# A Fourier transform and a two-layer network on one core: the first batch in two wide chunks instead of three narrow ones

## The chip, the core and the metric

The kernel runs on one NeuronCore of a Trainium2 chip. The core has five engines with a queue of their own each, which run side by side and wait for one another through semaphores: TensorE (matrix multiplications into PSUM; PE in the profile, its weight loads PEld), VectorE (DVE), ScalarE (ACT), GpSimd (POOL) and SyncE (SP), which here only issues DMAs. Every engine works through its instructions in the order in which the program gives them. The metric is the device time of one execution in microseconds (us); lower is better.

## The reference

```python
X = np.fft.fft(np.fft.fft(x, axis=1), axis=2)      # x: 8 x 3008 x 256, float32
x = X.real.astype(np.float32).reshape(8 * 3008, 256)
h = x @ w_in                                       # 256 x 2048
g = np.maximum(0.01 * h, h)
return (g @ w_out).astype(np.float32)              # 2048 x 256
```

The real part of a two-dimensional Fourier transform (over sequence and features) of eight batches, then a linear layer, a leaky ReLU and a second linear layer for each of the 24064 rows. The weights arrive as 64-bit floats.

## The kernel before

**Transform.** Each batch is transformed along the sequence in two units, the odd rows and the even rows of the result (`units`; 753 and 752 columns in all). A unit is made by folding the input (sums and differences, "x folds"), small matmuls against tables, and a butterfly of sums on VectorE into `mix_sb`; a separate row for the middle ("Nyquist") feature goes through DRAM and is broadcast into `nb_sb`. The feature transform is folded into `w_in`, which gives `wf`.

**Columns.** The first 504 columns of batch 0 are done by plain steps: sixteen pairs (j, f), `steps`, where `raised` (R) makes the hidden sums of two hidden blocks in four PSUM half banks, `activate` (A) adds the middle row, makes sum and difference on VectorE and the leaky ReLU on ScalarE, and `down_plain` (D0 and D1, the two halves of the output) multiplies by `wo`. A Lrelu of an A inside the first chunk is not issued at once but put into the list `waiting`, and goes out after the next up.

All other columns are done by chunks (`Chunk`). Each has 16 "ups" (`up`, L1235: one matmul for the cosine and one for the sine part over the chunk's width w), with the cosine bank seeded beforehand by ScalarE (`seed`, L1230), copied out by ScalarE (L1241) and combined with the sine bank by VectorE (`hidden`, L1248, two operations, the "hidden pair"), then a Lrelu (L1511). Then a fast multiplication scheme: 28 sums of the hidden values on VectorE and GpSimd (`sum`, L1265), 26 products of four matmuls with n = w/2 columns (`product`, L1286), and combinations on VectorE (L1332). The weights of the products are sums of `w_out` blocks, made by GpSimd (W, L736), stored to DRAM (L741) and streamed back (L760).

**Order.** Nothing is left to a scheduler: every engine gets its instructions in program order. `HEAD` is a written list of operations ahead of the first chunk. `rest` then sorts events by a step number: chunk t has its ups at steps 16t + 1.2 + f and its products from 16t + 18.1 on, beside the next chunk's ups. `START` is a table of further operations at the beginning of steps. The background work for the next batches (`work`, x folds and transforms) is put in by budgets per step (`SHARES`). The letters of `HEAD` and `START` mean: L load a weight part; C finish converting one part from 64-bit floats and begin the next (B, M, E are pieces of it); S and F fold a quarter of `w_in` into `wf` (S two sums, F matmuls on TensorE, L708, and four ScalarE copies, L712); T, N, NF tables and the middle row; W the weight sums of one group.

A conversion C is five VectorE operations (L651, L643, L644, L660, L661); the two ScalarE ones of the part that is begun (L645, L646) wait for L644.

**Banks.** Ups use `cos_ps` and `sin_ps`, two banks each. In the first chunk, for the ups f < `EARLY`, `half` gives bank 0 alone, since the plain steps and F use bank 1; then the two alternate. `seed_next` seeds the next up only after the copy of this one while f < `EARLY`. Where a chunk is wider than all before it, `touch` (L1226) first runs a small matmul over the new columns of both banks.

**Before, batch 0:** the chunks have 248, 380 and 373 columns (n = 124, 190, 187); the transform of its second unit is done inside the first chunk (in `start_work`, steps 5 to 13), which holds only columns of the first unit. All other batches have three chunks of 504, 504 and 497. That makes 24 chunks.

Of the kernel before, what the change touches and what calls it, by code (L numbers as in the profile page):

```python
# [16 lines left out]
P = 128  # L17
# [23 lines left out]
CW = 252  # L41
# [21 lines left out]
    15: "D0:15",  # L63
    16: "D1:15",
    17: "",
# [4 lines left out]
L:o3 D0:0 R:1 B:o1 D1:0 A:2 R:3 C:o1 A:1 A:3 D0:2 L:w2a C:w1a C:w1b D1:2 D0:1 L:w2b S:1 D1:1 D0:3 F:1 D1:3 R:4 C:o2 L:o4 L:o5 A:4 C:o3 R:5 A:5 D0:4 C:w2a D1:4 R:6 L:w3a A:6 D1:5 T C:w2b D0:5 R:7 D0:6 A:7 S:2 L:w3b L:o6 F:2 C:o4 D1:6 R:8 A:8 N D1:7 R:9 C:o5 D0:7 A:9 R:10 NF C:w3a D0:8 A:10 L:o7 D0:9 C:w3b R:11 S:3 D1:9 W:1 D1:8 W:0 A:11 F:3  # L70
"""
EARLY = 14
FIRST_DOWN = 18.1
FIRST_PER = 6.5
RF = 128
SHARES = (0.9, 1.2, 1.34)
DIRECT = (11, 13)
WORK_FROM = 14
FOLDS_FROM = 16
FIRST = 125  # L80
# [54 lines left out]
SECOND = 380  # L135
# [195 lines left out]
def tile_fnet_leaky_relu(  # L331
# [41 lines left out]
    def ring(tag):  # L373
# [5 lines left out]
    assert weights_at >= lay_out(block_sb, 0, (("win", 4, WN), ("power", 2, WN), ("raw", 1, 2 * WN), ("e", 2, 2 * WN), ("o", 2, 2 * WN),  # L379
                                               ("g", 5, 2 * WN), ("s", 4, 2 * WN)))  # L380
# [96 lines left out]
    def turn(x, y, a, part, tmp, to, v, sc=None):  # L477
# [4 lines left out]
        if v is folds:  # L482
# [110 lines left out]
    feat_sb = in_parts(2 * 2 * P, 2, 2 * P, where="cos")  # L593
# [15 lines left out]
    RAW = "o e raw o e o e raw o e o e raw o e raw".split()  # L609
# [117 lines left out]
    def weight(w):  # L727
        if w >= 8:
            return wt[:, w - 8]
# [46 lines left out]
    stream = Stream()  # L776
    reach = [w % 4 for w in range(8)]
    for x_, y_, _ in W_SUMS:
        reach.append(max(reach[x_], reach[y_]))

# [277 lines left out]
    class Later:  # L1058
# [4 lines left out]
        def __init__(self):  # L1063
            self.queue, self.turn, self.alone = [], 0, 0
# [65 lines left out]
    class Slots:  # L1130
# [3 lines left out]
        def __init__(self):  # L1134
            self.under = {SLOTS + i: {4 * RF * i // SS, (4 * RF * (i + 1) - 1) // SS} for i in range(16)}
            self.free = set(range(SLOTS)) - set().union(*self.under.values())
# [16 lines left out]
        def drop(self, i):  # L1153
            if i in self.under:
                freed = self.under.pop(i)
                self.free |= freed - set().union(*self.under.values())
            else:
                self.free.add(i)

        def place(self, i, n):  # L1160
            if i >= SLOTS:
                return block_sb[:, (i - SLOTS) * 4 * RF : (i - SLOTS + 1) * 4 * RF].rearrange("p (g n) -> p g n", g=4)[:, :, 0:n]
            return block_sb[:, i * SS : i * SS + 4 * RS].rearrange("p (g n) -> p g n", g=4)[:, :, 0:n]

        def row(self, r, g, n):
            if r[0] >= SLOTS:
                all_of = block_sb[:, 0 : 64 * RF].rearrange("p (i n) -> p i n", n=4 * RF)
                return all_of[:, r[0] - SLOTS : r[-1] + 1 - SLOTS, g * RF : g * RF + n]
# [32 lines left out]
    class Chunk:  # L1201
# [18 lines left out]
        def half(self, f):  # L1220

            return 0 if self is every[0] and f < EARLY else f % 2

# [8 lines left out]
        def up(self, f):  # L1232
# [5 lines left out]
            if g == 0:  # L1238
                self.at.update(zip(range(4 * k, 4 * k + 4), block.take_four() if self is not every[0] else range(SLOTS + 4 * k, SLOTS + 4 * k + 4)))
# [122 lines left out]
    def step_of(b, i, r):  # L1362

        return 16 * (3 * b + i) + r
# [53 lines left out]
    def rest():  # L1418
# [99 lines left out]
    def start_work(r):  # L1518
# [4 lines left out]
        if r == 5:  # L1523
            store_weights(range(8))
        if r in (6, 7):
            store_weights([8 + i for last in ((1, 0), (2, 3))[r - 6] for i in range(len(W_SUMS)) if reach[8 + i] == last])
        if r == 10:
            stream.load_to(5)
        if r == 17:
            stream.load_to(RING)  # L1530
        if r in (5, 7):
            part = (r - 5) // 2
            fold_halves(t, part, 0, slice(0, 2 * FI))
            evens.append(Direct(t[:, part, 0, :, part * P : (part + 1) * P], part, even_tables[part], 0))
        if r in (8, 10):
            evens[(r - 8) // 2].fold_odd(t[:, (r - 8) // 2, 1, 0:2, 0:P])
        if r == 9:
            rings["dft"] = rings["up"]
            nyq_t = nyquist_tile()
            made = butterfly(nyquist_halves(nyq_t, 0), B, 0, 0)  # L1540
            made[0](even_rows(nyq_of[0], B))
            made[1](odd_rows(nyq_of[0], B))
            store_nyquist(0, nyq_t)
            spread(1)
        if r in DIRECT:
            dft_direct(DIRECT.index(r))

# [11 lines left out]
    def do(op, later=None):  # L1559
# [36 lines left out]
        elif kind == "NF":  # L1596
# [4 lines left out]
            nyq_of.append(rows)  # L1601
        else:
# [146 lines left out]
```

## Time and profile before

| | us |
|---|---|
| median of 3 runs (lowest, highest) | 1816.27 (1816.03, 1816.39) |
| profiled execution, its own time | 1816.45 |
| its span, from the first to the last instruction | 1814.3 |
| TensorE busy in the span | 1806.7 |
| VectorE busy | 1537.6 |
| ScalarE busy | 1065.0 |
| GpSimd busy | 1036.3 |
| first up of chunk 0, 1, 2, 3 begins at | 94.3, 138.6, 181.1, 239.0 |

A row of the timeline has the start, the time to the end of the last of the merged instructions, engine, line, operation, output and inputs, shape, count, and in brackets the idle time ahead of it and what ended it. A matmul of 32-bit floats appears as two records, and the end of a record is modelled: the next matmul starts before it. So the cost of a matmul is read from one start to the next.

### The profile page before, as it was taken

What the parts mean: (1) busy time and instruction counts of PE and PEld (TensorE: products, weight loads), DVE (VectorE), ACT (ScalarE), POOL (GpSimd) and SP (SyncE); (2) the same over time, 40 slices, a digit from 0 to 9 for tenths busy, and PEclk for the clock granted to TensorE, in tenths of its full rate; (3) what the DMA queues carried; (4) which work ended last, traced back from release to release, by engine and by line L of the source; (5) the groups of instructions that cost most, each with busy time, mean ns of one, the idle gap of its engine ahead of it and who ended that gap; (6) DMA issues with size and microseconds to landing.
All of it is one profiled execution on the core that took longest, in us unless ns stands there. A gap on an engine that the chain in (4) does not pass through costs nothing.

```text
span 1814.3 us, 23376 instructions
## 1 busy us (share of the span) xinstructions
PE 1806.7 (100%) x7512; PEld 1358.3 (75%) x7512; DVE 1537.6 (85%) x2684; ACT 1065.0 (59%) x1891; POOL 1036.3 (57%) x461
## 2 busy tenths in 40 slices
PE   9999999999999999999999999999999999999999
PEld 7788877777777777777777777777777777777778
DVE  8879988897788987999878989689887997886868
ACT  4768666665556655666556655566555665555540
POOL 0156656565566655755656656566566566565730
PEclk9999999999999999999999999999999999999999
DMA  7366454533454333633436234443443533323324
GB/s 249 108 236 220 135 166 140 176 112 101 132 175 143 121 99 116 214 99 125 130 122 203 90 121 135 149 159 100 133 131 130 175 120 118 121 90 104 126 90 153
DMA packets 148872, 252.49 MB, mean 139 GB/s; under 512 B 18944, under 2 KB 55424, under 8 KB 148752
## 3 DMA queue, kind: packets, MB, share of 16 engines
q1 hardware_dynamic: 148608, 251.02, 42.0%
q8 instruction: 60, 0.98, 0.2%
q14 instruction: 60, 0.49, 0.1%
q10 hardware_dynamic: 144, 0.00, 0.0%
HBM read 219.41 MB, written 31.54 MB: 138 GB/s over the span
## 4 chain that ended last, share of the span: by engine, by line
PE 96%; DVE 3%; issue 0%; POOL 0%; ACT 0%; DVEq 0%; POOLq 0%
PE sum_psc L1286 21%; PE sum_psa L1286 17%; PE sum_psb L1286 17%; PE cos_psa L1235 9%; PE sin_psa L1235 9%; PE cos_psb L1235 8%; PE sin_psb L1235 8%; PE dft_ps L813 3%; DVE block L1265 1%; PE sum_psa L1610 1%; PE dft_ps L1050 1%; DVE block L1026 0%; PE sum_psb L1050 0%; PE sum_psc L1050 0%; PE sum_psa L1050 0%
## 5 line engine op out<-in xcount | busy, mean ns | idle before, releaser
L1265 POOL TENSOR_TENSOR block<-block 128x1008 f32<-128x1008 f32 (+4 forms) x414 | 996.1, 2417 | 640.4 <-DVE xt L1071 172.0
L1286 PE MATMUL sum_psc<-block,wr 128*128 128x252 f32 (+4 forms) x1912 | 428.0, 367 | 0.1
L1286 PEld LDWEIGHTS sum_psc<-block,wr 128*128 128x128 f32 x1912 | 353.8, 190 | 92.2 <-issue 58.2
L1265 DVE TENSOR_TENSOR block<-block 128x1008 f32<-128x1008 f32 (+4 forms) x258 | 415.7, 1615 | 0.3
L1511 ACT ACTIVATE block<-block 128x504 f32<-128x504 f32 (+7 forms) x556 | 399.0, 747 | 4.4 <-DVE block L1248 4.2
L1248 DVE TENSOR_TENSOR block<-cos,sin_psa 128x504 f32<-128x504 f32 (+4 forms) x398 | 238.5, 640 | 148.9 <-PE sin_psa L1235 145.6
L1286 PE MATMUL sum_psb<-block,wr 128*128 128x252 f32 (+4 forms) x1536 | 349.5, 367 | 0.0
L1286 PE MATMUL sum_psa<-block,wr 128*128 128x252 f32 (+4 forms) x1544 | 346.3, 367 | 0.1
L1286 PEld LDWEIGHTS sum_psb<-block,wr 128*128 128x128 f32 x1536 | 282.4, 190 | 83.6 <-issue 53.5
L1286 PEld LDWEIGHTS sum_psa<-block,wr 128*128 128x128 f32 x1544 | 285.1, 190 | 66.4 <-issue 38.8
L1248 DVE TENSOR_TENSOR block<-cos,sin_psb 128x504 f32<-128x504 f32 (+4 forms) x370 | 228.3, 658 | 92.8 <-PE sin_psb L1235 90.7
L1241 ACT COPY cos<-cos_psa 128x504 f32<-128x504 f32 (+4 forms) x199 | 110.2, 554 | 257.9 <-PE cos_psa L1235 257.9
L1241 ACT COPY cos<-cos_psb 128x504 f32<-128x504 f32 (+4 forms) x185 | 105.0, 567 | 228.1 <-PE cos_psb L1235 227.9
L1235 PE MATMUL cos_psa<-mixc,wf 128*128 128x504 f32 (+4 forms) x398 | 190.6, 561 | 0.5 <-ACT cos_psa L1230 0.5
L1235 PE MATMUL sin_psa<-mixs,wf 128*128 128x504 f32 (+4 forms) x398 | 190.5, 560 | 0.0
L1332 DVE TENSOR_TENSOR part<-part 128x252 f32<-128x252 f32 (+4 forms) x357 | 187.8, 563 | 1.4
L1235 PE MATMUL cos_psb<-mixc,wf 128*128 128x504 f32 (+4 forms) x370 | 182.2, 574 | 0.0
L1235 PE MATMUL sin_psb<-mixs,wf 128*128 128x504 f32 (+4 forms) x370 | 182.2, 574 | 0.0
L1235 PEld LDWEIGHTS sin_psa<-mixs,wf 128*128 128x128 f32 x398 | 75.4, 190 | 82.5 <-issue 63.2
L1230 ACT ACTIVATE cos_psa<-nb,small 128x504 f32<-128x504 f32 (+4 forms) x199 | 131.2, 659 | 7.5 <-PE cos_psa L1226 1.2
L1235 PEld LDWEIGHTS sin_psb<-mixs,wf 128*128 128x128 f32 x370 | 70.3, 190 | 81.7 <-issue 66.1
L1230 ACT ACTIVATE cos_psb<-nb,small 128x504 f32<-128x504 f32 (+4 forms) x185 | 124.5, 673 | 7.1 <-PE cos_psb L1226 1.2
(203 smaller groups left out, 1348.1 us busy)
## 6 DMA issues: line engine op xcount, KB each, us to landing
wr<-w_dram SPq DMA_DIRECT2D x600, 256.0 KB, 3.4
xt<-in_x_dram SPq DMA_DIRECT2D x28, 1024.0 KB, 7.3
out_dram<-part SPq DMA_DIRECT2D x112, 126.0 KB, 1.8
out_dram<-part SPq DMA_DIRECT2D x56, 124.5 KB, 1.9
tabe<-in_seq_tab_dram SPq DMA_DIRECT2D x29, 190.0 KB, 3.9
w_dram<-block SPq DMA_DIRECT2D x18, 256.0 KB, 3.6
block<-in_w_in_dram SPq DMA_DIRECT2D x8, 512.0 KB, 4.7
block<-in_w_out_dram SPq DMA_DIRECT2D x8, 512.0 KB, 4.5
```

The source lines that it names most:

```text
L813: nc.tensor.matmul(o, lhsT=still, rhs=moving, start=(i == 0), stop=(i == 3), skip_group_check=True)
L1050: nc.tensor.matmul(sums[j][d][:, r * n : (r + 1) * n], lhsT=wo[:, fs[h] // 4, fs[h] % 4, d], rhs=a[r][h], start=(f == 0 and r == 0 and h = ...
L1230: nc.scalar.activation(cos_ps[self.half(f)][:, 0 : self.w], nb_sb[:, self.lo : self.lo + self.w], ACT.Copy, scale=wn[:, f : f + 1])
L1235: nc.tensor.matmul(bank[:, 0 : self.w], lhsT=wf[:, i, f * P : (f + 1) * P], rhs=mix_sb[i][:, self.lo : self.lo + self.w], start=(i == 1), ...
L1241: nc.scalar.copy(copy, cos[:, 0 : self.w])
L1248: nc.vector.tensor_tensor(block.row(to, g, self.n), x, y, op=op)
L1265: ins = (engine or nc.gpsimd).tensor_tensor(self.value(16 + i), xa, ya, op=ALU.add if sign > 0 else ALU.subtract)
L1286: nc.tensor.matmul(to, lhsT=stream.weight(self.t, q, g), rhs=self.value(v)[:, g], start=(first and at == 0), stop=(last and g == 3), skip_ ...
L1332: ins = nc.vector.tensor_tensor(part_of[self.copy[v]][:, 0:n], xa, ya, op=ALU.add if sign > 0 else ALU.subtract)
L1511: nc.scalar.activation(to, to, ACT.Lrelu)
L1610: nc.tensor.matmul(pt[:, 0:columns], lhsT=blank[:, 0:P], rhs=blank[:, 0:columns], start=True, stop=True)
```

## The change

Batch 0 gets two chunks of 504 and 497 columns like the other batches (23 chunks in all). The first one now begins in unit 0 and ends in unit 1, so the second unit's transform (Q, Y and X, formerly in `start_work`) moves into `HEAD`. In exchange the last quarter of `w_in` (C:w3a, C:w3b, S:3, F:3) moves from `HEAD` into the first steps of the first chunk, and the plain steps R:12 to R:15 with their A and D move some steps back. The load of batch 1's input goes from step 14 to step 1, and its folds begin at step 8. Up f = 4 of the first chunk uses bank 1 (`ASIDE`). The hidden values of the first chunk lie in ordinary slots of `block_sb` (`FIRST_SLOTS`), and the head's buffers there are laid out anew. Until step 17 the x folds use no PSUM copies (`folds.copies`): both inputs are in SBUF. The weight sums are stored in two parts, at steps 3 and 11. The diff is cut to what the prediction speaks of.

```diff
 START = {
-    0: "C:o6 D0:10 R:12 A:12",
-    1: "D1:10 M:o7",
-    2: "R:13 A:13",
-    3: "D0:11 E:o7 D1:11 W:2 W:3",
-    4: "R:14 A:14",
-    5: "D0:12",
-    6: "R:15 A:15",
-    7: "D1:12",
-    8: "D0:13",
-    9: "D1:13",
-    10: "D0:14",
-    12: "D1:14",
-    15: "D0:15",
+    0: "C:w3a D0:10",
+    1: "L:o7 D1:10",
+    2: "C:w3b D0:11",
+    3: "S:3 D1:11",
+    4: "F:3",
+    5: "C:o6",
+    6: "M:o7 E:o7",
+    7: "R:12 A:12 W:3",
+    8: "D0:12",
+    9: "D1:12",
+    10: "R:13 A:13",
+    11: "R:14 A:14",
+    12: "D0:13",
+    13: "D1:13 D0:14",
+    14: "R:15 A:15",
+    15: "D1:14 D0:15",
     16: "D1:15",
-    17: "",
 }
...
-... D1:7 R:9 C:o5 D0:7 A:9 R:10 NF C:w3a D0:8 A:10 L:o7 D0:9 C:w3b R:11 S:3 D1:9 W:1 D1:8 W:0 A:11 F:3
+... D1:7 R:9 C:o5 D0:7 A:9 R:10 NF Q:0 D0:8 A:10 Q:1 W:2 D0:9 R:11 Y D1:9 A:11 X:0 D1:8 X:1
...
-EARLY = 14
+EARLY, ASIDE = 14, 4
-SHARES = (0.9, 1.2, 1.34)
-DIRECT = (11, 13)
-WORK_FROM = 14
-FOLDS_FROM = 16
+SHARES = (2.4, 1.6, 1.34)
+WORK_FROM = 1
+FOLDS_FROM = 8
...
+FIRST_SLOTS = [(14, 15, 16, 17), (10, 11, 12, 13), (6, 7, 8, 9), (18, 19, 20, 21)]
...
-    ends = [PLAIN * CW, UW[1], UW[1] + SECOND, sum(UW)]
-    for lo, hi in zip(ends, ends[1:]):
-        add(0, lo, hi)
-    for b in range(1, B):
-        for lo in range(0, sum(UW), WIDE):
+    for b in range(B):
+        for lo in range(0 if b else PLAIN * CW, sum(UW), WIDE):
             add(b, lo, min(lo + WIDE, sum(UW)))
...
         def by_turns(self, to, x, y, op):
             self.turn = (self.turn + 1) % TURNS
+            if not self.copies:
+                return self.tensor_tensor(to, x, y, op)
...
-            return 0 if self is every[0] and f < EARLY else f % 2
+            return int(f == ASIDE) if self is every[0] and f < EARLY else f % 2
...
-        return 16 * (3 * b + i) + r
+        return 16 * (3 * b + i - 1) + r
...
-                now[0] = SHARES[0] if 16 * t + i < 34 else SHARES[1] if 16 * t + i < 48 else SHARES[2]
+                now[0] = SHARES[0] if 16 * t + i < 17 else SHARES[1] if 16 * t + i < 32 else SHARES[2]
...
-        if r == 5:
+        if r == 3:
+            store_weights([w for w in by_reach if reach[w] == 2])
+        if r == 8:
             store_weights(range(8))
-        if r in (6, 7):
-            store_weights([8 + i for last in ((1, 0), (2, 3))[r - 6] for i in range(len(W_SUMS)) if reach[8 + i] == last])
-        if r == 10:
+        if r == 11:
+            store_weights([w for w in by_reach if reach[w] == 3])
+        if r == 13:
             stream.load_to(5)
         if r == 17:
+            folds.copies = True
+            block.free |= block.later
             stream.load_to(RING)
-        if r in (5, 7):
...
+        elif kind == "Q":
+            part = int(at)
+            fold_halves(t, part, 0, slice(0, 2 * FI))
+            evens.append(Direct(t[:, part, 0, :, part * P : (part + 1) * P], part, even_tables[part], 0))
+            evens[part].fold_odd(t[:, part, 1, 0:2, 0:P])
+        elif kind == "X":
+            dft_direct(int(at))
+        elif kind == "Y":
+            pt = raw[steps[PLAIN * NH - 5]]
+            assert cos_ps[0] in pt
+            rings["dft"] = [0, [i for i in rings["up"][1] if i not in pt]]
...
+            store_nyquist(0, nyq_t)
+            spread(1)
```

More of the change, by code (lines that the diff above doesn't have):

```diff
@@ L481, in turn @@
         sc = nc.scalar if sc is None else sc
-        if v is folds:
+        if v is folds and folds.copies:
             tmp = [misc_ps[0:ROWS, (2 * a + i) % 4 * P : ((2 * a + i) % 4 + 1) * P] for i in range(2)]
@@ L779, in tile_fnet_leaky_relu @@
         reach.append(max(reach[x_], reach[y_]))
+    by_reach = sorted(range(8, len(reach)), key=lambda w: reach[w])
+    stream = Stream()
     def even_rows(rows, m):
@@ L1063, in __init__ @@
         def __init__(self):
-            self.queue, self.turn, self.alone = [], 0, 0
+            self.queue, self.turn, self.alone, self.copies = [], 0, 0, False
         def tensor_tensor(self, to, x, y, op):
@@ L1134, in __init__ @@
         def __init__(self):
-            self.under = {SLOTS + i: {4 * RF * i // SS, (4 * RF * (i + 1) - 1) // SS} for i in range(16)}
-            self.free = set(range(SLOTS)) - set().union(*self.under.values())
+            self.free = set(range(FIRST_SLOTS[3][3] + 1, SLOTS))
+            self.later = set(range(FIRST_SLOTS[2][0]))
         def take(self):
@@ L1238, in up @@
             if g == 0:
-                self.at.update(zip(range(4 * k, 4 * k + 4), block.take_four() if self is not every[0] else range(SLOTS + 4 * k, SLOTS + 4 * k + 4)))
+                self.at.update(zip(range(4 * k, 4 * k + 4), block.take_four() if self is not every[0] else FIRST_SLOTS[k]))
             copy = cos_sb[:, f % 2, 0 : self.w]
```

46 lines of the change are left out of this document (11 added, 35 removed).

## The prediction, made before the changed kernel was run

> **What bounds the kernel now.** I read the page first, then busy time by stage, then TensorE in order of time around the first chunks. Times are us, from the span's start.
>
> ```profile
> span 1814.3 us, 23376 instructions
> PE 1806.7 (100%) x7512; PEld 1358.3 (75%) x7512; DVE 1537.6 (85%) x2684; ACT 1065.0 (59%) x1891; POOL 1036.3 (57%) x461
> PE 96%; DVE 3%; issue 0%; POOL 0%; ACT 0%; DVEq 0%; POOLq 0%
> ```
>
> TensorE is the chain. A change can win only by taking matmul time away or by removing its gaps, and it loses where it makes gaps. The first chunk (up matmuls from 94.27) and everything from the first chunk of batch 1 on, in the view of stages:
>
> ```profile
> 94.27:139.00 44.73, 44.05 (x215) 37.49 (x214) 32.74 (x78) 28.11 (x60) 24.54 (x19) 1.00 0.69 243
> 239.00:1814.00 1575.00, 1571.72 (x6348) 1166.14 (x6346) 1330.30 (x2256) 905.96 (x1585) 933.22 (x376) 1.00 0.40 132
> ```
>
> From 239 on TensorE never stands, though DVE (third figure) is busy 84% of it. That part isn't edited, so the difference is made before it. The gaps there, in TensorE's timeline:
>
> ```profile
> 130.20 0.58 PE L1235 MATMUL sin_psa<-mixs,wf 128*128 128x248 f32 x2
> 131.32 0.69 PE L1235 MATMUL cos_psa<-mixc,wf 128*128 128x248 f32 x2 [0.54 <-ACT cos_psa L1230]
> ...
> 134.51 0.58 PE L1235 MATMUL sin_psa<-mixs,wf 128*128 128x248 f32 x2
> 135.13 0.49 PE L1226 MATMUL cos_psa<-mixc,wf 128*128 128x132 f32 x2
> 135.46 1.86 PE L1050 MATMUL sum_psb<-block,wr 128*128 128x252 f32 x8
> ```
>
> The first pair shows the pattern that decides my forecast. The first chunk keeps to one pair of banks, so an up waits until ScalarE has copied the cosine bank and seeded it anew (L1230); without other matmuls between two ups TensorE stands. Only 0.5 of such waiting is in the profile now.
>
> **Removed: narrow chunks.** Product matmuls (two records each), starts of consecutive groups:
>
> ```profile
> 168.65 1.50 PE L1286 MATMUL sum_psb<-block,wr 128*128 128x124 f32 x12
> 169.99 0.39 PE L1286 MATMUL sum_psc<-block,wr 128*128 128x124 f32 x2
> ...
> 236.75 1.46 PE L1286 MATMUL sum_psb<-block,wr 128*128 128x190 f32 x8
> 238.04 1.13 PE L1286 MATMUL sum_psc<-block,wr 128*128 128x190 f32 x6
> ...
> 307.98 3.14 PE L1286 MATMUL sum_psa<-block,wr 128*128 128x252 f32 x14
> ...
> 310.95 1.01 PE L1235 MATMUL cos_psa<-mixc,wf 128*128 128x504 f32 x2
> ```
>
> A record costs 1.34/12 = 0.1117 at 124 columns, 1.29/8 = 0.161 at 190, 2.97/14 = 0.212 at 252. The columns are the same before (124 + 190 + 187 = 501) and after (252 + 249). From 190 to 252 a column costs 0.00082, so 187 costs 0.1588 and 249 costs 0.2097. Three chunks: 0.4315; two: 0.4217. The 0.0098 is saved 208 times: 2.0. The ups keep their 1002 columns and lose 64 records at the fixed few ns, within that figure's rounding. **-2.0.**
>
> The touches (L1226) run where a chunk is wider than all before it; now the first is the widest, so all four go. Each costs 135.46 - 135.13 = 0.33 and the gap ahead, here 135.13 - (134.51 + 0.42) = 0.2, elsewhere 0.1 to 0.26: **-2.0** for four. The wait at 130.62 goes with the narrow chunk (0.7, and two delayed issues of 0.1): **-0.9**. Together -4.9.
>
> **Moved, costed near nothing.** The second unit's transform (Q, Y, X) goes from the first chunk into the head with its matmuls unchanged; the last quarter's fold and R:12 go the other way. Unit 1's final sums must now be ready before the first up:
>
> ```profile
> 121.27 1.44 PE L554 MATMUL cos_psb<-block,xt 128*128 128x378 f32 x6
> ...
> 123.84 0.58 PE L1235 MATMUL cos_psa<-mixc,wf 128*128 128x248 f32 x2
> ```
> ```profile
> 124.57 0.67 DVE L887 TENSOR_TENSOR mixc<-half,sin_psb 128x189 f32<-128x189 f32 x3
> ```
>
> One X is 2.57 on TensorE, and VectorE ends 1.4 behind it. D0:10 and D1:10 (1.70 each, eight records of 0.212) stand between X:1 and the first up, and cover that; without them it would cost 1.4. The nyquist row's store and broadcast have D1:9, X:0, D1:8 and X:1 (8.5) as cover. For odd issue delays **+0.3**, bounds 0 and 1.4. On SyncE's queue, the input of batch 1 (from step 14 to 1) and the first weight sums' stores (step 3) go ahead of the small copies behind F:3:
>
> ```profile
> 104.58 13.07 SPq L741 DMA_DIRECT2D w_dram<-block  x18
> ```
>
> Seven stores issue in 7 x 0.73 = 5.1, well before A:12 needs those copies in step 7. The first x folds have 7 steps for their load. The later half of batch 1's first transform falls into the second chunk, whose load is like that of the stage from 239 on: 0, bounds 0 and +1.
>
> **Moved, and not covered: the waits in the first wide chunk.** Its steps have TensorE work as the new table lists it: 16 ups, ten half-downs, four R and F:3. The prices at the new width are in the later chunks:
>
> ```profile
> 302.59 1.01 PE L1235 MATMUL cos_psa<-mixc,wf 128*128 128x504 f32 x2
> 303.44 1.01 PE L1235 MATMUL sin_psa<-mixs,wf 128*128 128x504 f32 x2
> 303.63 0.58 ACT L1241 COPY cos<-cos_psa 128x504 f32<-128x504 f32 x1 [1.45 <-PE cos_psa L1235]
> 304.25 0.69 ACT L1230 ACTIVATE cos_psa<-nb,small 128x504 f32<-128x504 f32 x1
> ...
> 305.38 1.04 ACT L1511 ACTIVATE block<-block 128x1008 f32<-128x1008 f32 x1
> ...
> 306.21 1.25 DVE L1248 TENSOR_TENSOR block<-cos,sin_psa 128x504 f32<-128x504 f32 x2
> ```
>
> An up is 2 x 0.845 = 1.69. The copy starts 1.04 after the cosine half and takes 0.58, the seed 0.69, a Lrelu 1.0, the hidden pair 1.25 (1.18 to the next). F and a conversion stand in the head, on TensorE, ScalarE and VectorE:
>
> ```profile
> 47.15 1.02 PE L708 MATMUL cos_psb<-block,cos 128*128 128x512 f32 x2
> ...
> 52.03 1.12 PE L1005 MATMUL sin_psa<-mixc,wf 128*128 128x252 f32 x4 [0.40 <-ACT sin_psa L997]
> ```
> ```profile
> 47.35 1.19 ACT L712 COPY wf<-sin_psa 64x512 f32<-64x512 f32 x2 [1.75 <-PE sin_psa L708]
> 48.44 1.17 ACT L712 COPY wf<-cos_psb 64x512 f32<-64x512 f32 x2
> 49.64 0.72 ACT L645 ACTIVATE block<-block,small 128x512 f32<-128x512 int32 x1
> 50.39 0.72 ACT L646 ACTIVATE block<-block,small 128x512 int32<-128x512 f32 x1
> 51.02 0.96 ACT L997 ACTIVATE sin_psa<-nb,small 128x252 f32<-128x252 f32 x2
> ```
> ```profile
> 46.78 0.69 DVE L651 SCALAR_TENSOR_TENSOR wr<-block,wr 128x512 f32<-128x512 uint32 x1
> ...
> 48.78 0.69 DVE L661 SCALAR_TENSOR_TENSOR wr<-wr,block 128x512 f32<-128x512 f32 x1
> ...
> 50.82 0.86 DVE L1018 SCALAR_TENSOR_TENSOR part<-nb,small,sin_psb 128x252 f32<-128x252 f32 x2 [1.35 <-PE sin_psb L1005]
> 51.79 1.27 DVE L1026 TENSOR_TENSOR block<-part,cos_psa 128x504 f32<-128x504 f32 x2
> ```
>
> So a C is 2.6 on VectorE, its two Relus 1.4 on ScalarE, F's four copies 2.2, an A 2.1 on VectorE. Here, too, the seed (L997) came behind copies and Relus, and TensorE waited at 52.03 although half-downs and an R lay between. I follow the three queues by these prices, with 0 at the first wide up:
>
> - *Step 3, 0.5.* C:w3b runs on VectorE 3.2 to 5.8; its Relus keep ScalarE until 5.95, so copy 1 and seed 2 end at 7.2, and up 2 could have begun at 6.8.
> - *Step 5, 1.45.* F:3 ends at 10.9. Behind its copies (to 12.7) stand copy 3 and seed 4, to 13.95. TensorE has only up 3, done at 12.6.
> - *Step 6, 2.95.* C:o6 waits on VectorE behind hidden pair 3 (to 14.55); its Relus end at 17.35, copy 4 and seed 5 at 18.6. Up 4 was done at 15.75, and steps 5 and 6 hold no half-down and no R.
> - *Step 8, 2.65.* E:o7 and hidden pair 5 hold VectorE to 22.3, A:12 to 24.45; its Lrelu, behind that of pair 5, ends at 26.35. D0:12 reads it, one step after A:12 instead of five; up 6 ended at 23.8.
> - *Step 15, 1.6.* A:15's Lrelu, behind two seeds and another Lrelu, ends at 55.05; D1:14 ended at 53.6.
>
> With 0.25 for small delays these give **+9.4**. Each row's duration is measured; that the order of the queues makes them add is worked out. Its bounds are 0 (ScalarE and VectorE are covered after all) and 12 (with the port, below).
>
> **Sum.** -4.9 + 0.3 + 9.4 = +4.8. The profiled execution took 1816.45, 2.15 of it outside the span; that makes 1821.25, and the median of the runs is 0.18 under it: **1821.0**.
>
> **Rivals.** *(1) ScalarE isn't late: faster.* If the Relus of C:w3b and C:o6 and F's copies come early enough that seed 4 and seed 5 are no more than half a us late, and D0:12 finds its Lrelu, only about 1.5 of waiting is left: 1816.27 - 4.9 + 0.3 + 1.5 = 1813.2. For it: half-downs and R cover ten of sixteen steps, and now nearly all is covered. Against it: steps 5 and 6 have nothing on TensorE but one up each. *(2) One wait pays for the next: no change.* While TensorE stands in steps 5 and 6 VectorE catches up, and the Lrelus ahead of D0:12 and D0:15 are done in time. 9.4 - 2.65 - 1.6 = 5.2 remain: 1816.9. Against it: A:12 comes behind E:o7 on VectorE, not behind TensorE. *(3) The port: slower still.* The x folds start in step 8 without their PSUM copies, so both inputs are in SBUF, while GpSimd makes the last eleven weight sums (W:3 in step 7). What that can cost, with GpSimd's sums beside the first row and not beside the second:
>
> ```profile
> 113.07 1.99 DVE L571 TENSOR_TENSOR xt<-xt 128x128 f32<-128x128 f32 x2
> ...
> 120.63 0.47 DVE L571 TENSOR_TENSOR xt<-xt 128x128 f32<-128x128 f32 x2
> ```
>
> That is 0.76 more for one operation. Eight folds in steps 8 and 9 would be 6 later on VectorE; half lies under the wait for D0:12 and the half-downs, so hidden pair 8 comes some 2.5 late: 1823.5. The Trainium skill, page "SBUF — State Buffer", section "SBUF: two separate sides", says why: VectorE with two SBUF inputs and GpSimd take the shared port in turn, each for a whole instruction. By that rule every one of these folds may wait out a GpSimd sum; the two rows agree with it.
>
> **Chances.** Forecast 0.44, (1) 0.12, (2) 0.31, (3) 0.13. A difference under 0.2% (3.6) can't be told from none. Faster takes (1) less its upper edge: 0.10; slower takes (3) and the forecast's part over 1819.9: 0.54; the rest, 0.36, is within. The forecast's own range is 1818 to 1823; the range 1813.5 to 1824.5 holds most of (1) and (3) too.
>
> **What would show it.** Right: in the first chunk TensorE idle before cos_psb and cos_psa (L1235), released by the seed L1230, of 1 to 3 us at the fifth and sixth up, and before sums (L1050) released by the Lrelu L1511; no L1226; 0 lost later. Wrong: less than 4 us of idle between the first up and the second chunk, or fresh idle in the head or the second chunk, where I count 0.3 and 0. The forecast fails first if the seeds of the fifth and sixth up come in time.

## The result, and the profile after

The changed kernel takes **1833.13 us** (median; lowest 1832.31, highest 1833.41), the kernel before 1816.38 in runs on the same chip. The ratio is 1.0091, 95% interval 1.0076 to 1.0106: slower by 16.7. The prediction, 1821.0 with a range of 1813.5 to 1824.5, had the direction and little over a quarter of the size.

The page of the changed kernel, and its view of stages for the first chunk (ups from 103.3 to 170.4) and for everything from batch 1's first chunk on (columns as before: TensorE, weight loads, VectorE, ScalarE, GpSimd, granted clock, DMA share, GB/s):

```profile
span 1830.5 us, 22511 instructions
PE 1808.5 (99%) x7232; PEld 1336.7 (73%) x7232; DVE 1543.0 (84%) x2608; ACT 1046.2 (57%) x1791; POOL 1034.6 (57%) x443
PE 93%; DVE 4%; ACT 1%; DMA 1%; issue 1%; SPq 0%; POOL 0%; DVEq 0%; POOLq 0%
```
```profile
103.30:170.40 67.10, 56.41 (x181) 34.35 (x181) 58.38 (x88) 45.16 (x66) 20.17 (x14) 0.97 0.60 206
244.10:1830.00 1585.90, 1582.95 (x6347) 1172.99 (x6345) 1337.18 (x2251) 904.52 (x1561) 949.85 (x380) 1.00 0.40 131
```

TensorE, 96% of the chain before, is 93% of it now. In the first chunk it stands 67.10 - 56.41 = 10.7 us, and in what remains the granted clock is 0.97; the later stage is as it was. So the loss lies in the head and the first chunk. TensorE's timeline there, the rows with a wait ahead of them (in brackets; "issue": none that the profile shows) and three without:

```profile
91.35 1.98 PE L550 MATMUL sin_psa<-block,xt 128*128 128x378 f32 x6 [3.67 <-issue]
...
110.58 1.11 PE L1225 MATMUL cos_psa<-mixc,wf 128*128 128x504 f32 x2 [0.30 <-ACT cos_psa L1220]
...
117.52 1.11 PE L1225 MATMUL cos_psb<-mixc,wf 128*128 128x504 f32 x2 [1.57 <-ACT cos_psb L1220]
...
122.07 1.20 PE L1225 MATMUL cos_psa<-mixc,wf 128*128 128x504 f32 x2 [2.60 <-ACT cos_psa L1220]
123.06 1.89 PE L1225 MATMUL sin_psa<-mixs,wf 128*128 128x504 f32 x2
124.74 1.83 PE L1002 MATMUL cos_psb<-mixc,wf 128*128 128x252 f32 x4
126.41 1.01 PE L1002 MATMUL sin_psb<-mixs,wf 128*128 128x252 f32 x4
...
131.55 1.97 PE L1047 MATMUL sum_psa<-block,wr 128*128 128x252 f32 x8 [2.44 <-ACT block L1501]
...
139.55 1.11 PE L1225 MATMUL sin_psa<-mixs,wf 128*128 128x504 f32 x2 [1.80 <-DVE block L1238]
...
143.66 1.11 PE L1225 MATMUL sin_psa<-mixs,wf 128*128 128x504 f32 x2 [0.46 <-DVE block L1238]
...
145.81 1.12 PE L1002 MATMUL sin_psb<-mixs,wf 128*128 128x252 f32 x4 [0.18 <-DVE block L1023]
...
163.53 1.97 PE L1047 MATMUL sum_psa<-block,wr 128*128 128x252 f32 x8 [1.34 <-ACT block L1501]
...
174.52 1.10 PE L1225 MATMUL sin_psb<-mixs,wf 128*128 128x498 f32 x2 [1.01 <-DVE block L1238]
```

Five of these waits are the five that the prediction named (steps 3, 5, 6, 8 and 15), at their places and released by the engines it named. Four things are beside them.

*The head, 91.35.* Ahead of X stands a wait of 3.67. VectorE's fold of the second unit (L440) in its two halves, Q:0 and Q:1, and the first two and the last two of GpSimd's seven weight sums W:2, of which all but the first run beside the second half:

```profile
78.58 0.95 DVE L440 TENSOR_TENSOR xt<-xt 128x768 f32<-128x768 f32 x1
...
82.12 7.65 DVE L440 TENSOR_TENSOR xt<-xt 128x768 f32<-128x768 f32 x1
```
```profile
80.33 2.51 POOL L732 TENSOR_TENSOR block<-wr 128x512 f32<-128x512 f32 x2
...
86.46 2.50 POOL L732 TENSOR_TENSOR block<-block,wr 128x512 f32<-128x512 f32 x2
```

The same operation takes 0.95 alone and 7.65 beside the sums, and it ends only when GpSimd has done all seven (88.96). The two operations just ahead of it, with one input in PSUM (L1023, 80.94), take 1.27 beside the first sums and 1.27 without them (77.39). Y's operations on VectorE are queued behind it, and X waits for them.

*The granted clock.* Three of the five-us stretches (the last but two columns is the clock):

```profile
85.00:90.00 5.00, 2.67 (x18) 1.98 (x15) 4.97 (x2) 1.14 (x4) 3.96 (x4) 1.00 0.00 0
90.00:95.00 5.00, 3.65 (x10) 2.83 (x11) 4.00 (x14) 1.42 (x3) 0.00 (x0) 0.72 0.03 5
...
120.00:125.00 5.00, 2.93 (x5) 1.42 (x6) 3.91 (x7) 4.61 (x8) 0.26 (x1) 0.80 0.25 67
```

After the wait in the head, and again after those of steps 5 and 6, TensorE runs at half speed for a while: above, the sine half begun at 123.06 takes 124.74 - 123.06 = 1.68 instead of 0.845, and the four records after it 1.67 instead of 0.85. Each such stretch costs 1.7. In the profile of before there is none after its first six us.

*Steps 9 to 11, 139.55.* The x folds (L1068) with both inputs in SBUF, five beside GpSimd's last weight sums and five without them:

```profile
130.40 7.91 DVE L1068 TENSOR_TENSOR xt<-xt 128x512 f32<-128x512 f32 x5
...
150.18 3.10 DVE L1068 TENSOR_TENSOR xt<-xt 128x512 f32<-128x512 f32 x5
```

0.96 more for each. *The second chunk, 174.52.* The turn (L1090), two operations on VectorE that also read SBUF twice, beside three block sums of GpSimd:

```profile
168.48 3.68 DVE L1090 SCALAR_TENSOR_TENSOR xt<-xt,small 95x128 f32<-95x128 f32 x2
```
```profile
167.35 8.12 POOL L1255 TENSOR_TENSOR block<-block 128x1008 f32<-128x1008 f32 x3 [26.68 <-PE sin_psa L1225]
```

The parts are counted on TensorE's records: from each start to the next, less what a record of that many columns takes in an undisturbed row (0.4225 at 504, 0.2125 at 252). Matmul time falls by 2.9, and the small waits of before at 130 to 139 and 232 to 237 (2.0) go. Against these -4.9 stand 5.4 in the head (3.7 of waiting, 1.7 at half clock), 9.6 in the five waits with their delayed issues, 1.7 at half clock behind steps 5 and 6, 3.2 in steps 9 to 11 and 1.3 in the second chunk: together **+16.3**; the span grew by 1830.5 - 1814.3 = 16.2. (The profiled execution is the shortest of the five, 1832.31.)

### The profile page after: what moved, and what is told of

Its sections match the earlier page's. It is cut to its first block, busy times and chain, and to the rows that moved or that the text cites. A ratio compares the mean times of both kernels' runs of the same rounds, so it can differ in the third digit from the quotient of the medians.

```text
span 1830.5 us, 22511 instructions
## 1 busy us (share of the span) xinstructions
PE 1808.5 (99%) x7232; PEld 1336.7 (73%) x7232; DVE 1543.0 (84%) x2608; ACT 1046.2 (57%) x1791; POOL 1034.6 (57%) x443
## 4 chain that ended last, share of the span: by engine, by line
PE 93%; DVE 4%; ACT 1%; DMA 1%; issue 1%; SPq 0%; POOL 0%; DVEq 0%; POOLq 0%
PE sum_psc L1276 21%; PE sum_psa L1276 17%; PE sum_psb L1276 17%; PE cos_psa L1225 8%; PE sin_psa L1225 8%; PE sin_psb L1225 8%; PE cos_psb L1225 8%; PE dft_ps L810 3%; DVE block L1255 1%; PE sum_psa L1605 1%; DVE block L1238 1%; DVE xt L1068 0%; DVE block L1023 0%; DMA w_dram<-block 0%; DVE part L1322 0%
## 5 line engine op out<-in xcount | busy, mean ns | idle before, releaser
L1255 POOL TENSOR_TENSOR block<-block 128x1008 f32<-128x1008 f32 (+1 forms) x396 | 994.2, 2522 | 633.2 <-DVE xt L1068 162.2
L1276 PE MATMUL sum_psc<-block,wr 128*128 128x252 f32 (+1 forms) x1832 | 425.9, 375 | 0.2 <-DVE block L1255 0.2
L1255 DVE TENSOR_TENSOR block<-block 128x1008 f32<-128x1008 f32 (+1 forms) x248 | 416.0, 1682 | 0.1
L1501 ACT ACTIVATE block<-block 128x504 f32<-128x504 f32 (+3 forms) x510 | 393.3, 798 | 2.7 <-DVE block L1238 2.4
L1238 DVE TENSOR_TENSOR block<-cos,sin_psa 128x504 f32<-128x504 f32 (+1 forms) x380 | 239.5, 671 | 159.0 <-PE sin_psa L1225 154.8
L1276 PE MATMUL sum_psb<-block,wr 128*128 128x252 f32 (+1 forms) x1472 | 346.9, 376 | 0.0
L1276 PE MATMUL sum_psa<-block,wr 128*128 128x252 f32 (+1 forms) x1480 | 344.9, 375 | 0.0
L1238 DVE TENSOR_TENSOR block<-cos,sin_psb 128x504 f32<-128x504 f32 (+1 forms) x356 | 224.2, 671 | 96.2 <-PE sin_psb L1225 94.8
L1225 PE MATMUL sin_psa<-mixs,wf 128*128 128x504 f32 (+1 forms) x380 | 192.1, 587 | 2.3 <-DVE block L1238 2.3
L1225 PE MATMUL cos_psa<-mixc,wf 128*128 128x504 f32 (+1 forms) x380 | 191.3, 585 | 2.9 <-ACT cos_psa L1220 2.9
```

Of the source, the lines that this page charges most:

```text
L1225: nc.tensor.matmul(bank[:, 0 : self.w], lhsT=wf[:, i, f * P : (f + 1) * P], rhs=mix_sb[i][:, self.lo : self.lo + self.w], start=(i == 1), ...
L1238: nc.vector.tensor_tensor(block.row(to, g, self.n), x, y, op=op)
L1255: ins = (engine or nc.gpsimd).tensor_tensor(self.value(16 + i), xa, ya, op=ALU.add if sign > 0 else ALU.subtract)
L1276: nc.tensor.matmul(to, lhsT=stream.weight(self.t, q, g), rhs=self.value(v)[:, g], start=(first and at == 0), stop=(last and g == 3), skip_ ...
L1501: nc.scalar.activation(to, to, ACT.Lrelu)
```

## The experiments

The theories: **(A)** GpSimd's weight sums shut out VectorE's operations with two SBUF inputs (the port), and each long gap costs half-clock time on top; **(B)** the late seeds of ScalarE, behind the conversions, F and E, make the first-chunk waits; **(C)** VectorE simply has too much to do in the first chunk, so that what is taken from one place comes back at another. Time lost on TensorE is in all 8.7 before and 28.0 after, by the count above; the matmuls that e2 adds (2.1) are not counted as lost.

| run | median (lowest to highest) | ratio, 95% interval | lost on TensorE |
|---|---|---|---|
| the change | 1833.13 (1832.31, 1833.41) | 1.0091 (1.0076, 1.0106) | 28.0 |
| e1 sums behind Y | 1826.84 (1826.31, 1827.12) | 1.0056 (1.0041, 1.0071) | 22.0 |
| e2 gap filled | 1832.82 (1831.62, 1833.16) | 1.0088 (1.0073, 1.0103) | 26.7 |
| e3 sums at step 10 | 1835.17 (1833.91, 1836.28) | 1.0102 (1.0087, 1.0117) | 32.0 |
| e4 weights in the head | 1826.33 (1825.54, 1828.57) | 1.0058 (1.0041, 1.0075) | 21.2 |
| e5 spread | 1823.98 (1823.61, 1824.37) | 1.0042 (1.0027, 1.0057) | 20.2 |
| e6 all in the head | 1822.90 (1822.67, 1825.83) | 1.0041 (1.0026, 1.0055) | 18.6 |
| e7 late turn | 1824.75 (1823.66, 1826.38) | 1.0046 (1.0031, 1.0061) | 21.3 |
| e8 copies covered | 1822.14 (1820.25, 1823.02) | 1.0030 (1.0018, 1.0041) | 18.9 |
| e9 turn in PSUM | 1821.40 (1819.58, 1822.67) | 1.0024 (1.0014, 1.0035) | 17.3 |
| e10 fewer folds at 8 | 1820.82 (1819.33, 1822.34) | 1.0023 (1.0014, 1.0032) | 17.0 |
| e11 border | 1820.91 (1820.42, 1821.34) | 1.0023 (1.0014, 1.0032) | 16.9 |
| e12 folds at 7 | 1819.50 (1819.21, 1821.43) | 1.0018 (1.0009, 1.0027) | 16.6 |

**e1, the weight sums W:2 behind Y.**

```diff
-... Q:0 D0:8 A:10 Q:1 W:2 D0:9 R:11 Y D1:9 A:11 ...
+... Q:0 D0:8 A:10 Q:1 D0:9 R:11 Y W:2 D1:9 A:11 ...   # GpSimd's first sum waits for Y's last VectorE operation
```

> The first seven weight sums on GpSimd (W:2) wait for the last VectorE operation of Y instead of running beside Q:1. If the long fold in Q:1 (7.65 us against 0.95 in Q:0) is VectorE shut out by those sums, it takes about 1 us here, TensorE's gap of 3.8 before the first X and the low clock behind it (1.7) go, and the time is 1833.1 - 5.5 = 1827.6. If the lateness is only taken over by the later waits of the first chunk, the fold is short but the time stays above 1831. If the fold was long for another reason, nothing changes: 1833.

Measured: 6.3 less. Its timeline of VectorE (Q:1), stages, and TensorE around the one stretch at half clock that is left:

```profile
81.77 0.95 DVE L440 TENSOR_TENSOR xt<-xt 128x768 f32<-128x768 f32 x1
```
```profile
85.00:90.00 5.00, 5.00 (x27) 4.12 (x26) 3.96 (x13) 2.34 (x7) 2.30 (x2) 1.00 0.03 5
90.00:95.00 5.00, 5.00 (x25) 4.23 (x24) 2.86 (x13) 0.90 (x2) 5.00 (x5) 1.00 0.26 77
```
```profile
124.16 2.78 PE L1047 MATMUL sum_psa<-block,wr 128*128 128x252 f32 x8 [2.44 <-ACT block L1507]
126.73 1.89 PE L1231 MATMUL cos_psa<-mixc,wf 128*128 128x504 f32 x2
128.41 1.10 PE L1231 MATMUL sin_psa<-mixs,wf 128*128 128x504 f32 x2
```

Q:1 is back to 0.95, TensorE never stands in the head, and the clock there stays at 1.00: (A) is shown for the head. The waits of the five steps are at least as long as in the change (0.73, 1.74, 2.76, 2.60, 1.51), so they do not come from the head. The half clock now follows the wait of step 8, and not that of step 6: the eight records of sums take 126.73 - 124.16 = 2.57 instead of 1.70 and the next half 1.68 instead of 0.845, 1.7 in all.

**e2, the gap of step 6 filled** with five matmuls of 256 columns that go to the free sine bank and are not used.

```diff
+        if r == 6:
+            for _ in range(5):
+                nc.tensor.matmul(sin_ps[0][:, 0 : 2 * P], lhsT=wf[:, 0, 0:P], rhs=mix_sb[0][:, 0 : 2 * P], ...)
```

> Five matmuls of 256 columns, whose result nobody uses, fill 2.1 us of TensorE's gap of 2.7 before the sixth up. If the clock of 0.80 and 0.86 in 120 to 130 comes from TensorE's standing still in 115 to 122, it stays at 1.00 and the next up and R:12 take their normal time: 1833.1 - 1.9 = 1831.2. If the clock does not depend on that gap, the time is 1833 to 1833.5.

Measured: no difference from the change. The stages of this run:

```profile
90.00:95.00 5.00, 3.82 (x8) 2.77 (x9) 4.00 (x14) 1.42 (x3) 0.00 (x0) 0.56 0.03 5
95.00:100.00 5.00, 5.00 (x20) 4.34 (x19) 1.50 (x7) 0.00 (x0) 0.00 (x0) 0.76 0.19 77
120.00:125.00 5.00, 4.56 (x16) 2.77 (x15) 4.28 (x8) 4.03 (x6) 0.00 (x0) 1.00 0.49 137
...
130.00:135.00 5.00, 3.93 (x10) 2.88 (x11) 5.00 (x5) 1.02 (x2) 4.92 (x4) 0.66 0.36 96
```

With the gap filled the clock stays at 1.00 there. In e1 it did so with the gap open (2.60), so that the filling is the reason is not shown. In this profile the clock falls after the next gap, that of step 8, instead, and in the head (0.56 and 0.76) it costs 3.1 instead of 1.7. Filling this one gap of several gained nothing.

**e3, W:3 from step 7 to step 10,** so that the folds of steps 8 and 9 run alone.

```diff
-    7: "R:12 A:12 W:3",
+    7: "R:12 A:12",
...
-    10: "R:13 A:13",
+    10: "R:13 A:13 W:3",
```

> The last eleven weight sums (W:3) begin at step 10 instead of 7. If they are what makes the x folds of steps 8 and 9 long (first five 7.9 us, 3.1 later for five), those folds take 0.6 each, the waits for hidden pairs after them (2.0, 0.6, 0.4) go, and the time is 1830 to 1831.5, the more the fewer folds of steps 12 and 13 meet the sums. If VectorE simply has too much to do in these steps, the folds stay long or the waits move and the time stays at 1833.

Measured: 2 more than the change, a miss. VectorE's folds, and two groups of TensorE's waits (total, times, longest):

```profile
130.21 3.10 DVE L1068 TENSOR_TENSOR xt<-xt 128x512 f32<-128x512 f32 x5
...
148.16 7.86 DVE L1068 TENSOR_TENSOR xt<-xt 128x512 f32<-128x512 f32 x5
```
```profile
PE sin_psa L1225 <- DVE block L1238: 2.7, 1, 2.7
PE sin_psb L1225 <- DVE block L1238: 2.0, 1, 2.0
```

Without the sums beside them the first five folds take 3.10 instead of 7.91, and steps 9 to 11 lose nothing: (A) holds there too. But now five others meet the sums at step 12 and TensorE waits 2.7 behind them, the second chunk waits 2.0 instead of 1.0, and there are two more stretches at half clock, one behind the wait of step 8 (0.75 at 130 to 135) and one in the second chunk (0.68 at 175 to 180). The clash was moved, not removed; some 3.4 of what this profile loses is those two stretches.

**e4, the last conversions back in the head,** with e1's order of W:2, and W:3 early.

```diff
-... R:10 NF Q:0 D0:8 A:10 Q:1 W:2 D0:9 R:11 Y D1:9 A:11 X:0 D1:8 X:1
+... R:10 NF C:w3a Q:0 D0:8 A:10 L:o7 Q:1 D0:9 C:w3b R:11 S:3 Y W:2 D1:9 A:11 X:0 D1:8 X:1 F:3
-    0: "C:w3a D0:10", 1: "L:o7 D1:10", 2: "C:w3b D0:11", 3: "S:3 D1:11", 4: "F:3", 5: "C:o6", 6: "M:o7 E:o7", 7: "R:12 A:12 W:3", ...
+    0: "C:o6 D0:10", 1: "D1:10 M:o7", 2: "E:o7 D0:11", 3: "D1:11 W:3", 4: "R:12 A:12", 5: "R:13 A:13", 6: "D0:12", 7: "D1:12", ...
```

> As e1_gate_sums, and the last quarter of the first weights is converted and folded in the head again, with plain steps R:12 and R:13 and half-downs spread so that nearly each step of the first chunk has one, and W:3 at step 3. If the waits come from the order on ScalarE and VectorE of conversions and copies ahead of the seeds (0.5, 1.8, 2.8, 2.6 and the low clock 1.9), about 9 go beyond e1's 5.5, W:3 no longer meets the folds (3), and the head loses 2 to 3 for its fuller VectorE: 1818 to 1820. If VectorE's total work up to the second chunk is the bound, the head takes the waits over: 1825 to 1828.

(R:13 at step 5 writes over the seed of the fifth up, which this run therefore leaves out of the sums; the instructions are the same.) Measured: no better than e1. Of the waits of steps 3 to 8 three of 0.3 to 0.6 are left, as (B) has it. But X waits 3.0 in the head, where VectorE is late behind the conversions, and the second up of chunk 1 waits 3.8 behind the turn, which again stands beside the block sums: what was won came back elsewhere, as (C) has it.

**e5 and e6, the conversions spread, or all of them with F:3 and two half-downs in the head,** Q:1 behind Y, W:2 last, the plain steps drawn forward, the fifth up on bank 0, the folds from step 9.

```diff
-... R:10 NF Q:0 D0:8 A:10 Q:1 W:2 D0:9 R:11 Y D1:9 A:11 X:0 D1:8 X:1
+... R:10 NF Q:0 D0:8 A:10 C:w3a L:o7 D0:9 R:11 Y Q:1 D1:9 A:11 X:0 C:w3b D1:8 X:1 S:3 W:2              # e5; F:3 in step 2, C:o6 in 3, E:o7 in 5, W:3 in 6
+... R:10 NF C:w3a Q:0 D0:8 A:10 L:o7 D0:9 R:11 Y Q:1 D1:9 A:11 X:0 C:w3b D1:8 X:1 S:3 D0:10 D1:10 F:3   # e6; C:o6 in step 0, W:2 in 1, E:o7 in 2, W:3 in 4
-EARLY, ASIDE = 14, 4
+EARLY, ASIDE = 14, 99
-FOLDS_FROM = 8
+FOLDS_FROM = 9
```

> All work of the changed kernel, another order. Head: C:w3a behind A:10, Q:1 behind Y, C:w3b behind X:0, S:3 and then the first weight sums behind X:1, so that no fold with two SBUF inputs meets them. First chunk: F:3, C:o6, M:o7 and E:o7 in steps of their own that also have a half-down or an R, no D in the step behind its A, all ups below 14 on bank 0, x folds from step 9. If the time of the changed kernel is lost to the order (ScalarE's queue 9.6, the port 3.8 and 3.1, the low clock 3.6), 12 to 15 of the 16.7 go: 1818 to 1821. If VectorE's sum of work ahead of the second chunk is the bound, its waits reappear as waits for hidden pairs (L1248's place) and the time stays at 1825 or more.

> As e5_spread, but C:w3a ahead of Q:0, and F:3 in the head behind D0:10 and D1:10, with C:o6, M:o7 and E:o7 in the first three steps and the weight sums W:2 from step 1 beside them. By the order theory the same 1818 to 1821, with 1 to 3 more where W:2 meets the last conversion; by the bound of VectorE's work 1825 or more.

Measured: 9 and 10 of the 16.7 come back. e5 lies between its two ranges; e6 is within the 1 to 3 more that its expectation allowed, though no wait in steps 2 to 8 shows the reason given there. In e5 the weight sums W:2, now last in the head, meet the conversion C:o6. A row of it, and TensorE's wait for the seed that came behind its Relus:

```profile
107.66 1.49 DVE L640 TENSOR_SCALAR block<-block 128x512 int32<-128x512 int32 x1
```
```profile
111.89 2.05 PE L1231 MATMUL cos_psa<-mixc,wf 128*128 128x504 f32 x2 [3.62 <-ACT cos_psa L1226]
```

L640 takes 0.42 without the sums (102.18 in the change). It has one input in SBUF, not two, so (A) as worded is too narrow; its output is in SBUF as well. The wait and a stretch at half clock behind it cost some 5.4, the largest loss in this run, and it is again a clash with the sums. In e6 nothing is lost in steps 3 to 8, but F:3's copies keep the first up's seed 2.0 late, eight folds around A:14 make one wait of 1.6, and VectorE, not ScalarE, sets the border of the two chunks: 1.2 before the first up of chunk 1 and 3.4 before the second.

**e7 and e8, from e6.** e7: no background work in step 17, folds from step 8. e8: also S:3 ahead of X:1, and F:3 between D0:10 and D1:10.

```diff
+                if 17 <= 16 * t + i < 18:
+                    now[0] = 0.0
...
-... X:0 C:w3b D1:8 X:1 S:3 D0:10 D1:10 F:3
+... X:0 C:w3b D1:8 S:3 X:1 D0:10 F:3 D1:10
-SHARES = (2.4, 1.6, 1.34)
+SHARES = (2.4, 2.4, 1.34)
```

> The order of the second rearranged head (last conversions, S:3, D0:10, D1:10 and F:3 in the head), with two edits: no background operation is given out at step 17, where GpSimd makes three block sums back to back, and the x folds begin one step sooner to make up for it. Port theory: the turn's two operations no longer run beside the block sums, so the wait of 3.4 before the second up of chunk 1 goes and most of the 1.2 ahead of it stays: 1819 to 1820. Rival (VectorE is simply full there, and what is put off comes back as a wait elsewhere): 1822 to 1824, with a wait of 2 or more in steps 8 to 16 or after step 18.

> As the run with the late turn, and in the head S:3 goes ahead of X:1 and F:3 between D0:10 and D1:10, so that F's four ScalarE copies have one half-down and GpSimd's sum for S:3 has X:1 and D0:10 beside them; the background share of VectorE in chunk 1 is 2.4 instead of 1.6. ScalarE theory: of the 3.3 lost about F:3 and the first up (0.50, 0.70 and 2.01) some 1.7 to 2.5 goes: 2 less than the run beside it. Rival (the copies only delay the seeds of the next ups): within 0.5 of the run beside it.

e7 missed and does not test what it was made for: with the folds begun earlier, the turn was given out a step earlier too, in step 16, and met the same three sums. e8 is 2.6 under e7; the intervals overlap, but the traces have the gain where it was expected: the losses about F:3 and the first up fall from 3.2 to 1.2 (ScalarE's copies are covered).

**e9, the turn's scaled copies in PSUM from the start,** from e8. In the kernel before they always went to the PSUM bank dft_ps; the change made that depend on `folds.copies`, which is set in step 17.

```diff
-        if v is folds and folds.copies:
+        if v is folds:
             tmp = [misc_ps[...] for i in range(2)]
```

> The run with the copies covered, with one edit: the turn's scaled copies always go to the PSUM bank dft_ps, as in the kernel before and in all later batches, so its scalar_tensor_tensor has one input in PSUM. Port theory: beside GpSimd's block sums the two operations take about 0.6 instead of 3.93, the wait of 3.94 before the second up of chunk 1 goes, and with it the granted clock of 0.65 in the ten us behind it (2.9 lost): 1822.1 - 4.9 - 2.5 = 1814.7, between 1814 and 1816. Rival (VectorE is only behind with its folds, and GpSimd has no part in it): the operations stay long or the wait goes to the next operation, 1820 to 1822.

VectorE in e8, then in e9, and GpSimd in e9:

```profile
156.41 3.93 DVE L1089 SCALAR_TENSOR_TENSOR xt<-xt,small 95x128 f32<-95x128 f32 x2
```
```profile
156.14 0.60 DVE L1089 SCALAR_TENSOR_TENSOR xt<-xt,small,dft_ps 95x128 f32<-95x128 f32 x2
157.62 3.31 DVE L1260 TENSOR_TENSOR block<-block 128x1008 f32<-128x1008 f32 x1 [0.89 <-POOL block L1260]
```
```profile
155.26 7.85 POOL L1260 TENSOR_TENSOR block<-block 128x1008 f32<-128x1008 f32 x3 [30.63 <-DMA wr<-w_dram]
```

The turn is cured, 0.60 instead of 3.93, with one input in PSUM and the same neighbour: (A) as a mechanism. The time is not, 1821.40 against an expected 1814.7: the next operation with two SBUF inputs, VectorE's own block sum (1.2 alone), first waits 0.89 for a block sum of GpSimd and then takes 3.31 beside the others, and the second up still waits 3.5. The time is (C)'s, but the operation that is late now is late beside the same sums, so this run does not speak against (A).

**e10 to e12, from e9.** e10 gives step 8, where A:14 stands, fewer folds, and step 17 its share again. e11 moves VectorE's first block sum of the border behind the second up of chunk 1, with no background work in steps 16 and 17, and for that begins the folds at step 6. e12 begins them at step 7.

```diff
+                if 16 * t + i in (8,):                       # e10, e11
+                    now[0] = 0.5
+                if 16 * t + i in (16, 17):                   # e11, e12
+                    now[0] = 0.0
-                events.append((16 * t + (s if t < count - 1 else ...), 1, t, i))
+                events.append((16 * t + (17.25 if (t, i) == (0, 3) else s if t < count - 1 else ...), 1, t, i))   # e11, e12
```

> As the run with the turn in PSUM, but step 17 gets its background work again, and step 8, where A:14 stands, gets a fifth of its x folds (0.5 instead of 2.4 of the share). If the wait of 2.00 before the sine half of the ninth up is VectorE's burst of A:14 and five folds, it goes and nothing else comes: 2 under the run beside it, 1812.5 to 1814. Rival (the folds come as a burst in the next step): within 0.7 of the run beside it.

> As the run with fewer folds at step 8, with three edits at the border of the two chunks: no background work is given out at steps 16 and 17, the fourth block sum (VectorE's, with both inputs in SBUF) goes behind the second up of chunk 1, and the x folds begin at step 6 with a share of 2.0, to be done by then. If the 4.6 lost at 154 to 161, and 1.8 lost to the clock behind it, come from work with two SBUF inputs that VectorE does ahead of the first two hidden pairs of chunk 1 while GpSimd makes block sums: 4 to 6 less, 1815 to 1817. Rival (VectorE and GpSimd have too much to do in these 12 us in any order): the wait moves by a step or two and 1819 to 1821 remains.

> As the run with the border of the chunks changed, but the x folds begin at step 7 instead of 6 (with a share of 2.2, and no smaller share at step 8), when GpSimd has at most three of its last weight sums left. Port theory: the four folds that took 5.83 beside those sums take 2.5 to 3.5, the wait of 2.58 at 122 shrinks to under 1 and the granted clock of 0.66 behind it is gone: 3 to 4 less, 1817 to 1818, of which a wait of some 1.5 at A:14 may come back: 1817 to 1819. Rival (the folds only move VectorE's lateness to the next step): 1820 to 1821.5.

e10 and e11 met their rivals' times, and e12 lies between its two ranges. In e10 the wait of 2.0 became two of 0.4 and 1.0, and the border waits as before. In e11 and e12 the border is mended, but the folds now meet the last weight sums. TensorE at the border in e11, VectorE's first four folds in e11, then in e12:

```profile
162.05 1.10 PE L1230 MATMUL cos_psb<-mixc,wf 128*128 128x498 f32 x2 [1.27 <-ACT cos_psb L1225]
```
```profile
118.17 5.83 DVE L1067 TENSOR_TENSOR xt<-xt 128x512 f32<-128x512 f32 x4
```
```profile
121.40 5.07 DVE L1067 TENSOR_TENSOR xt<-xt 128x512 f32<-128x512 f32 x4
```

The border's waits fell from 4.6 to 1.4, and four folds that take 2.5 alone take 5.83 and 5.07. e9 to e12 lie within each other's intervals and all above the kernel before: the best, 1819.50, is still 3.0 slower (1.0009 to 1.0027). No order tried here beats it. That none exists is not shown.

## Why the prediction was wrong

- *Removed, -4.9:* right. Matmul time fell by 2.9, and the waits with the touches by 2.0.
- *The waits in the first wide chunk, +9.4:* right in place and size. Predicted 0.5, 1.45, 2.95, 2.65 and 1.6; measured without the delayed issues 0.47, 1.74, 2.76, 2.60 and 1.51. The rule behind them (follow ScalarE's and VectorE's queues by the durations of rows, with TensorE's work as cover) carries. Rivals (1) and (2) are refuted: all five waits came in full, and none paid for the next. That they come from the conversions and copies is shown by e4 and e6, where these stand in the head and at most 0.6 of any wait in steps 3 to 8 is left. In step 8 the size is partly luck: the prediction let VectorE hold back the Lrelu of A:12, but A:12 was done at 128.85, and on ScalarE two rows tell what came first:

```profile
128.30 0.58 ACT L1231 COPY cos<-cos_psa 128x504 f32<-128x504 f32 x1 [2.73 <-PE cos_psa L1225]
...
129.53 1.96 ACT L1501 ACTIVATE block<-block 128x1008 f32<-128x1008 f32 x2
```

The two Lrelus (pair 5 and A:12) came behind the copy of up 6 and the seed of up 7, and that copy had waited for TensorE, which was late by its stretch at half clock. Both paths happen to give 2.6.
- ***Moved, costed near nothing*, +0.3 with bounds 0 and 1.4, is the step that failed.** The head lost 5.4. I followed Q, Y and X along TensorE, looking for cover behind X:1, and did not look at what stands beside them: `W:2` was moved in between Q:1 and Y in the same line of `HEAD`. The row for the port was quoted (L571, 1.99 beside the sums), and e1 shows that the sums beside Q:1 are the cause: without them 6.3 come back. The prediction's own sign of being wrong, fresh idle in the head and the second chunk, is what came. The size could not have been read from the rows, though. The profile of before has this same fold twice beside GpSimd's weight sums:

```profile
105.73 1.12 DVE L444 TENSOR_TENSOR xt<-xt 128x768 f32<-128x768 f32 x1
...
110.80 1.69 DVE L444 TENSOR_TENSOR xt<-xt 128x768 f32<-128x768 f32 x1
```

By these rows Q:1 would have cost 0.2 to 0.7 more, not 6.7. Why the same neighbours cost so much more here stays open.
- *The port, rival (3), +2.5:* it came, and it did not exclude the forecast. Steps 9 to 11 lost 3.2. I made a rival of what was a term of the sum. A fold costs 0.96 more beside the sums; I had 0.76.
- *Second chunk, 0 with bounds 0 and +1:* measured 1.3. The turn lost its PSUM copies with the same flag as the folds, and I counted it only for the folds.
- *The clock:* no term at all. Behind its first six us the profile of before has no gap over 0.9 us, and so no row that would show half speed behind a wait; two stretches at half clock cost 1.7 each, the first of them counted with the head.

The five missed terms, 5.1 in the head, 3.2, 1.3, 1.7 and 0.2 in the waits, make up the 11.5 between +4.8 and +16.3. The gains that were expected were real; the work that was moved was priced by itself and not with its new neighbours. What e4 to e12 add, argued from the sum of their places rather than shown by one run: VectorE is busy 58.38 of 67.10 in the first chunk, and so each order that spares one place makes another late. But some 6 of these 58 are themselves folds held up beside GpSimd's sums (7.91 and 3.02 for five and three of them, against 3.10 and 1.89). No run leaves GpSimd's sums out, so whether (A) or (C) keeps the last 3 us is not shown.

## What to carry to other kernels

For each operation that is moved, write down what the other engines do in the same microseconds, in both places; a price from a row holds only with the row's neighbours, and even the same neighbours do not fix it (the fold of 128x768: 1.12 and 1.69 before, 7.65 in the change). A term that does not depend on the forecast's being wrong belongs into the sum and not among the rivals. And where a change opens gaps of 2 us or more on TensorE, expect that some of them, not all, cost some 1.7 us more for a stretch at half clock; filling one gap of several won nothing in the one run that tried it.

## What was not expected of the hardware

**One operation can be shut out for six others.** Q:1, begun at 82.12, waited out the GpSimd sum that was under way and the five behind it, which themselves were not slowed (1.25 each), where the folds of steps 8 and 9 and the last sums took turns. GpSimd's sums beside those folds:

```profile
131.01 1.72 POOL L732 TENSOR_TENSOR block<-block,wr 128x512 f32<-128x512 f32 x1
132.69 1.71 POOL L732 TENSOR_TENSOR block<-wr,block 128x512 f32<-128x512 f32 x1
```

Here each sum takes 1.72 and each fold 1.6 on average. The Trainium skill, page "SBUF — State Buffer", section "SBUF: two separate sides", calls the port that VectorE with two SBUF inputs and GpSimd share an exclusive lock for a whole instruction. The turns agree with it, and so does e9 (one input in PSUM: 0.60). The section does not say who gets the lock next; why five sums that began after Q:1 all went ahead of it stays open, and no run here tells. The prediction had read the rule as taking turns, which holds for the folds and not for Q:1.

**The clock falls after gaps under 3 us, and not after each.** Most stretches at half speed cost about 1.7, that is 3.4 us of it (about 3 in the head of e2 and in e7 and e8). They came after a gap of 2.44 in e1, 2.42 in e11 and 3.67 in the head of the change, while a gap of 2.60 in e1 (step 6) and one of 3.24 in e6 were followed by none. One kernel even differs from execution to execution: seven of e12's eleven took 1819.21 to 1819.54 at a mean granted clock of 1.000, and four took 1820.65 to 1821.43 at 0.999; the profiled one, 1820.89, has one such stretch. The Trainium skill, page "TensorE: Matmul & The Clock Gate", section "Part 1: The HAM clock gate", gives half rate after at least one idle window of about 3.4 us, in windows that run freely. Half rate and the length of a stretch agree; that the gap must be as long as a window does not, since shorter ones sufficed here. That some gaps pass and others do not, and that executions of one kernel differ, would fit windows whose phase the kernel doesn't choose; it is not shown.
